# Threshold attention before a squared-ReLU feed-forward: shared last-query units, two units at a time, 64x64 tiles

## The chip, the cores and the metric

The kernel runs on one core of a Trainium2 chip. The metric is the device time of one execution in microseconds, from the first instruction to the last. The kernel before takes 1461.16 us (median of three runs, 1460.78 to 1461.53).

The engines are named as in the profile: PE (TensorE, matrix products and transposes), PEld (its weight loads), DVE (VectorE), ACT (ScalarE), POOL (GpSimd) and SP, which here only issues DMA. Each takes its own instructions in the order in which they were written and waits at semaphores for the others. Products land in PSUM, eight banks of 512 fp32 columns on 128 partitions; PE, DVE and ACT reach it here, POOL works on SBUF alone.

## What is computed

The reference has two parts. Attention, over 8 batches, 8 heads, 576 positions and head size 64:

```python
scores = scale * np.matmul(q, k.transpose(0, 1, 3, 2))
thresh = np.max(scores, axis=-1, keepdims=True) - tau
scores = np.where(scores >= thresh, scores, -1000000000.0)
scores = scores - np.max(scores, axis=-1, keepdims=True)
attn = np.exp(scores)
attn = attn / (np.sum(attn, axis=-1, keepdims=True) + 1e-09)
return np.matmul(attn, v).astype(np.float32)
```

Its result is laid out as 4608 tokens of 512 features, and a feed-forward follows: `h = max(x @ w_in, 0)`, then `(h * h) @ w_out`, with 2048 hidden features. q, k, v and the result are fp32, and the two weight matrices arrive as 64-bit floats. The number 576 is four and a half times 128, so each head has 64 queries and 64 keys left over after four full blocks; much of the kernel, and the whole change, is about these.

## The kernel before, in words

**The order of the work** is written out by hand. Attention comes first and ends when the first matmul of the feed-forward (`hidden_layer`, L708) starts; then come the nine steps of the hidden layer and the nine of the output layer (L843). The feed-forward uses a two-level scheme of sums in place of some products (`inner`, `sums`, `prepare_x`); the change leaves it alone, apart from when its weights are prepared during attention.

**Attention** goes over 32 pairs of heads. A pair has five slots (`slots`): four of 128 queries with both heads, and one of the last 64 queries, in which the two heads lie on the two halves of the partitions. That makes 160 slots. A slot passes these steps:

- `scores_rest` (L340): one full-array product of the 128 queries with a block-diagonal matrix of the last 64 keys of both heads (`kdiag`), into the middle of a three-bank PSUM tile `sc`, of which there are two.
- `scores` (L355): one product of 64 rows by 512 keys for each head. The heads sit on rows 0 to 63 and 64 to 127 of the array; in the last slot each uses 64 columns too.
- `softmax`: a negated maximum for each head on DVE (L366), the threshold on POOL (L371), exp on ACT (L378), mask and sum in one DVE instruction (L383), the small constant added on POOL (L387), a reciprocal on DVE (L389), and the normalization on POOL (L398).
- `transposes`: four 128-key transposes for each head (L439), and one for the last keys of both (L414), each into a PSUM bank that ACT then copies to SBUF (L441, L418). All use `bank`, a pool of two banks.
- `values` (L469, L474): ten products of 64 stationary columns, each head on its own half of the array's columns, with the last keys' values block diagonal (`vdiag`). They wait in `pending`, and the next slot's `rest` copies them out with its own transposes.

`turn` (L306) transposes q and k of the next pair once in five slots, and `turn_last` (L317) their last 64 rows. `load` and `load_v` fetch q, k and v. `slot(n)` interleaves all of this: it turns the weights of slot n-1, multiplies the values of slot n-2, and writes the scores of slot n+3, while `stage` and `second` step the softmaxes of n+1 and n+2. The engines run through the resulting queues; PE meets scores, values and transposes of different slots in a fixed sequence.

Between them lie the **weights of the feed-forward**: they arrive as 64-bit floats; `fetch` loads 32 raw tiles, `convert1` to `convert6` turn each into fp32 by ACT, POOL and DVE, and `sums_step` adds them on POOL, one addition a slot. `starts`, `OUT_SUMS`, `IN_FIRST` and `IN_SUMS` say in which slot each begins. The result x of attention goes to DRAM (`give_x`, `later`, `ask`), from where `load_x` takes it.

Of the kernel before, what the change touches and what calls it, by code (L numbers as in the profile page):

```python
# [48 lines left out]
def kernel(  # L49
# [74 lines left out]
    vdiag = [sb.tile([P, P], FP32, tag=f"vdiag{i}") for i in range(2)]  # L124
    kdiag = [sb.tile([P, P], FP32, tag=f"kdiag{i}") for i in range(2)]
    for t in vdiag + kdiag:
        nc.gpsimd.memset(t[:, :], 0.0)

# [137 lines left out]
    loaded, loaded_v, turned, weights = {}, {}, {}, {}  # L266

    def load(i):
        b, hp = pairs[i]
        h = 2 * hp  # L270
        qn = sb.tile([P, FULL, P], FP32, tag="qn", name="qn")
        kn = sb.tile([P, FULL, P], FP32, tag="kn", name="kn")

        rn = sb.tile([P, P], FP32, tag="rn", name="rn")

        for src, dst, order, rows in ((q, qn, "(t p) d -> p t d", 0), (k, kn, "(p t) d -> p t d", REST)):

            queue = nc.scalar if i == 0 and src is k else nc.sync
            for j in range(2):
                queue.dma_start(out=dst[:, :, ds(j * D, D)], in_=src[b, h + j, 0:MAIN, :].rearrange(order, p=P))  # L280
            queue.dma_start(
                out=rn[ds(rows, REST), :].rearrange("p (j d) -> p j d", j=2),
                in_=src[b, h : h + 2, MAIN:S, :].rearrange("j p d -> p j d"),
            )
        loaded[i] = (qn, kn, rn)

    def load_v(i):
        b, hp = pairs[i]
        h = 2 * hp
        va = sb.tile([P, 2, FULL, D], FP32, tag="va", bufs=2, name="va")  # L290
        vd = vdiag[i % 2]
        nc.sync.dma_start(out=va[:, :, :, :], in_=v[b, h : h + 2, 0:MAIN, :].rearrange("j (p t) d -> p j t d", p=P))
        for j in range(2):
            nc.sync.dma_start(out=vd[ds(j * D, D), ds(j * D, D)], in_=v[b, h + j, MAIN:S, :])
        loaded_v[i] = (va, vd)

    def turn(i):

        qn, kn, rn = loaded.pop(i)
        qT = sb.tile([P, S], FP32, tag="qT", bufs=2, name="qT")  # L300
        kT = sb.tile([P, S], FP32, tag="kT", bufs=2, name="kT")
        turning[i] = (qT, kT, rn)
        for nat, to in ((qn, qT), (kn, kT)):
            pt = bank([P, FULL, P], "pqk")
            for t in range(FULL):
                nc.tensor.transpose(pt[:, t, :], nat[:, t, :], ident[:, :])  # L306
            flat, to = pt[:, :, :].rearrange("p t m -> p (t m)"), to[:, 0:MAIN]
            if nat is kn:
                nc.scalar.copy(to, flat)
            else:  # L310
                nc.scalar.activation(out=to, in_=flat, func=AF.Identity, scale=qscale[:, :])
            yield

    def turn_last(i, pt):

        qT, kT, rn = turning.pop(i)
        nc.tensor.transpose(pt, rn[:, :], ident[:, :])  # L317

        def then():
            nc.scalar.activation(out=qT[:, MAIN:S], in_=pt[:, 0:REST], func=AF.Identity, scale=qscale[:, :])  # L320
            nc.scalar.copy(kT[:, MAIN:S], pt[:, REST:P])
            for j in range(2):
                rows = ds(j * D, D)
                nc.gpsimd.tensor_copy(out=kdiag[i % 2][rows, ds(j * REST, REST)], in_=kT[rows, MAIN:S])
            turned[i] = (qT, kT)
            if i + 1 < len(pairs):
                load(i + 1)
# [3 lines left out]
    def scores_rest(i, t):  # L331

        sc = sc_pool.tile([P, 3 * BANK], FP32, tag="sc", name="sc")
        if t < FULL:
            qT, _ = turned[i]
            to = sc[:, MAIN:S]
            to = bass.AP(tensor=to.tensor, offset=to.offset, ap=[to.ap[0], [2 * BANK - S, 2], [1, REST]])
            nc.tensor.matmul(to, qT[:, ts(t, P)], kdiag[i % 2][:, :], start=True, stop=True)  # L340
        return sc

    def scores(i, t, sc):

        qT, kT = turned[i]
        m = BLK[t]  # L350
        for k0, n in ((0, MAIN),) if t < FULL else ((0, MAIN), (MAIN, REST)):
            for j in range(2):
                rows = ds(j * D, D)
                to = sc[rows, ds(k0, n)] if t == FULL else sc[:, ds(j * 2 * BANK, n)]
                nc.tensor.matmul(to, qT[rows, ds(t * P, m)], kT[rows, ds(k0, n)], start=True, stop=True)  # L355

    def softmax(i, t, sc):

        nj = 2 if t < FULL else 1
        at = (0, 2 * BANK - REST)[0:nj]  # L360
        sm = sb.tile([P, 2], FP32, tag="sm", bufs=3, name="sm")
        nmx = sb.tile([P, 2], FP32, tag="nmx", bufs=3, name="nmx")
        thr = sb.tile([P, 2], FP32, tag="thr", bufs=3, name="thr")
        w = sb.tile([P, 2 * S], FP32, tag="w", bufs=3, name="w")
        for j in range(nj):
            nc.vector.tensor_reduce(  # L366
                out=nmx[:, j : j + 1], in_=sc[:, ds(at[j], S)], axis=AXIS.X, op=ALU.max, negate=True
            )
            if j == nj - 1:

                nc.gpsimd.tensor_scalar(  # L371
                    out=thr[:, 0:nj], in0=nmx[:, 0:nj], scalar1=-1.0, scalar2=tau_p[:, :], op0=ALU.mult, op1=ALU.subtract
                )
            yield
        for j in range(nj):
            if j:
                yield
            nc.scalar.activation(  # L378
                out=w[:, ts(j, S)], in_=sc[:, ds(at[j], S)], func=AF.Exp, bias=nmx[:, j : j + 1], scale=1.0
            )  # L380
        for j in range(nj):
            yield
            nc.vector.scalar_tensor_tensor(  # L383
                out=w[:, ts(j, S)], in0=sc[:, ds(at[j], S)], scalar=thr[:, j : j + 1], in1=w[:, ts(j, S)],
                op0=ALU.is_ge, op1=ALU.mult, accum_out=sm[:, j : j + 1],
            )
        nc.gpsimd.tensor_scalar(out=sm[:, 0:nj], in0=sm[:, 0:nj], scalar1=1e-9, scalar2=None, op0=ALU.add)  # L387
        yield
        nc.vector.reciprocal(out=sm[:, 0:nj], in_=sm[:, 0:nj])  # L389
        if t == FULL:  # L390

            normalize(w[:, S : S + REST], w[:, MAIN:S], sm[:, 0:1])
        for j in range(nj):
            normalize(w[:, ts(j, S)], w[:, ts(j, S)], sm[:, j : j + 1])
        weights[i, t] = w

    def normalize(out, w, r):
        nc.gpsimd.tensor_scalar(out=out, in0=w, scalar1=r, scalar2=1.0, op0=ALU.mult, op1=ALU.mult)  # L398

    def transposes(n):  # L400

        if n < 0:
            return
        i, t = slots[n]
        w = weights.pop((i, t))
        wT = sb.tile([P, 2, FULL, P], FP32, tag="wT", bufs=2, name="wT")
        weights[i, t] = wT
        at = ds(0, BLK[t])

        def rest():  # L410
# [8 lines left out]
            else:  # L419
                if n_:  # L420
                    nc.scalar.copy(xr[:, 0, 0:n_], pt[:, 0, 0:n_])
# [625 lines left out]
```

## Time and profile before

| what | value |
|---|---|
| time, median of three | 1461.16 us |
| span of the profiled execution | 1460.0 us |
| first scores product (L355) starts | 10.5 us |
| last scores product starts | 648.6 us |
| first feed-forward product (L708) starts | 661.5 us |
| one slot of attention, from two pairs in 40 us | 4.00 us |
| mask, mean (L383) | 814 ns, x288 |
| maximum, mean (L366) | 756 ns, x288 |
| exp, mean (L378) | 746 ns, x288 |
| 512-column copy of weights, mean (L441) | 592 ns, x256 |
| normalization, mean (L398, 576 columns) | 752 ns, x288 |
| granted TensorE clock | 1.00 |

How to read it: the profile lists groups of instructions by line, engine and shape with a mean duration. An engine starts its next instruction before the last has ended, so the distance between two starts in the timeline is the better measure of what an instruction costs its engine, and the mean tells when its result is there. Matmuls are pipelined, and their ends are modelled; only their starts are measured. The timeline merges runs of alike instructions into one line: start, duration, engine, line of the kernel, what it writes and reads, count, and, in brackets, how long the engine had been idle and for whom.

### The profile page before, as it was taken

The numbers are of one execution on the slowest core, as the hardware profiler recorded it, in microseconds if no ns is written. First come the engines' busy times: TensorE is split into PE (matmuls) and PEld (weight loads), VectorE is DVE, ScalarE is ACT, GpSimd is POOL, SyncE is SP. The second block draws the span as 40 slices with busy tenths as digits, with TensorE's granted clock in tenths as the row PEclk, the third lists the DMA queues.
The fourth block names the chain that finished last, engine by engine and source line by source line (L and its number), as shares of the span: only waits on it lengthen the run. The fifth ranks groups of instructions, "written<-read, shape, count | busy, mean of one in ns | idle before, by whom it ended". The sixth has DMA issues, their size and how long they took to land. (4 is left out here: it accounts for less than half of the span.)

```text
span 1460.0 us, 35321 instructions
## 1 busy us (share of the span) xinstructions
PE 1435.8 (98%) x12914; PEld 1216.0 (83%) x12914; DVE 1007.1 (69%) x2152; ACT 890.8 (61%) x1792; POOL 1053.6 (72%) x1318
## 2 busy tenths in 40 slices
PE   8999999999999999999999999999999999999998
PEld 5666666666666666669999999999999999999998
DVE  4888766777887667666777877778765656545663
ACT  5888777778887777774766666767543333323330
POOL 3777788778888888773556655666777777777775
PEclk9999999999999999999999999999999999999999
DMA  4443223676442222202433233433984442244411
GB/s 126 106 129 109 66 65 115 189 229 183 122 123 75 54 54 65 64 26 63 145 124 132 94 109 123 146 123 119 387 303 146 145 131 78 89 138 145 145 30 30
DMA packets 212957, 176.90 MB, mean 121 GB/s; under 512 B 99888, under 2 KB 161328, under 8 KB 212784
## 3 DMA queue, kind: packets, MB, share of 16 engines
q1 hardware_dynamic: 210896, 174.09, 38.0%
q8 instruction: 102, 1.67, 0.5%
q10 hardware_dynamic: 1888, 0.56, 0.2%
q14 instruction: 71, 0.58, 0.1%
HBM read 105.12 MB, written 69.47 MB: 120 GB/s over the span
## 5 line engine op out<-in xcount | busy, mean ns | idle before, releaser
L133 POOL TENSOR_TENSOR arena<-arena 128x512 f32<-128x512 f32 (+1 forms) x314 | 376.8, 1223 | 250.4 <-DVE arena L133 221.1
L708 PE MATMUL ph<-arena,w 128*128 128x128 f32 x3528 | 396.6, 275 | 1.5 <-DVE arena L133 0.5
L708 PEld LDWEIGHTS ph<-arena,w 128*128 128x128 f32 x3528 | 394.7, 192 | 3.4 <-DVE arena L133 2.9
L843 PE MATMUL po<-w,arena 128*128 128x128 f32 x3528 | 396.6, 275 | 0.3
L843 PEld LDWEIGHTS po<-w,arena 128*128 128x128 f32 x3528 | 394.9, 192 | 2.0 <-issue 1.6
L133 DVE TENSOR_TENSOR arena<-ph,arena 128x512 f32<-128x512 f32 x378 | 255.4, 688 | 93.0 <-PE ph L708 52.3
L366 DVE TENSOR_REDUCE arena<-sc 128x1 f32<-128x576 f32 x288 | 217.6, 756 | 127.9 <-PE sc L355 127.7
L383 DVE SCALAR_TENSOR_TENSOR arena<-sc,arena 128x576 f32<-128x576 f32 x288 | 224.6, 814 | 7.2 <-ACT arena L378 6.9
L398 POOL TENSOR_SCALAR arena<-arena 128x576 f32<-128x576 f32 (+1 forms) x320 | 223.6, 709 | 7.4 <-DVE arena L389 2.6
L133 DVE TENSOR_TENSOR arena<-po,arena 128x128 f32<-128x128 f32 x378 | 108.2, 290 | 169.5 <-PE po L843 168.3
L654 ACT COPY c<-arena 128x512 f32<-128x512 f32 (+1 forms) x303 | 172.9, 580 | 62.9 <-DVE arena L130 56.8
L378 ACT ACTIVATE arena<-sc,arena 128x576 f32<-128x576 f32 x288 | 200.6, 746 | 10.7 <-DVE arena L366 6.4
L439 PEld LDWEIGHTS pwT<-ident,arena 128*128 128x128 f32 x1152 | 128.6, 141 | 76.1 <-issue 29.9
L355 PE MATMUL sc<-arena 64*128 64x512 f32 (+2 forms) x768 | 184.5, 571 | 1.1 <-DVE arena L383 0.7
L130 POOL TENSOR_TENSOR arena<-arena 128x512 f32<-128x512 f32 (+1 forms) x138 | 175.0, 1268 | 9.7
L439 PE MATMUL pwT<-ident,arena 128*128 128x128 f32 x1152 | 180.9, 280 | 0.5 <-ACT arena L441 0.3
L130 DVE TENSOR_TENSOR arena<-arena,c 128x512 f32<-128x512 f32 (+1 forms) x267 | 174.9, 663 | 7.5 <-ACT c L654 6.6
L441 ACT COPY arena<-pwT 128x512 f32<-128x512 f32 x256 | 151.5, 592 | 42.0 <-PE pwT L439 31.7
L469 PE MATMUL pvR<-arena 128*64 128x128 f32 (+1 forms) x2560 | 163.3, 268 | 5.1 <-ACT arena L441 0.7
L469 PEld LDWEIGHTS pvR<-arena 128*64 128x64 f32 x2560 | 127.8, 136 | 34.8 <-issue 20.8
L687 ACT ACTIVATE arena<-arena 128x512 f32<-128x512 f32 x144 | 90.0, 625 | 76.8 <-POOL arena L133 76.7
L622 ACT COPY arena<-po 128x128 f32<-128x128 f32 x63 | 16.7, 265 | 179.0 <-PE po L843 177.1
(56 smaller groups left out, 1158.1 us busy)
## 6 DMA issues: line engine op xcount, KB each, us to landing
g<-arena SPq DMA_DIRECT2D x144, 256.0 KB, 2.0
arena<-g SPq DMA_DIRECT2D x144, 256.0 KB, 4.5
w<-w SPq DMA_DIRECT2D x98, 256.0 KB, 4.9
out_dram<-arena SPq DMA_DIRECT2D x70, 128.0 KB, 2.3
arena<-in_q_dram SPq DMA_DIRECT2D x64, 128.0 KB, 2.7
arena<-in_v_dram SPq DMA_DIRECT2D x32, 256.0 KB, 2.8
arena<-in_moe_w_out_dram SPq DMA_DIRECT2D x16, 512.0 KB, 4.2
xT<-arena SPq DMA_DIRECT2D x128, 64.0 KB, 1.6
```

The source lines that it names most:

```text
L130: e.tensor_tensor(out=out, in0=x, in1=y, op=ALU.subtract)
L133: e.tensor_tensor(out=out, in0=x, in1=y, op=ALU.add)
L355: nc.tensor.matmul(to, qT[rows, ds(t * P, m)], kT[rows, ds(k0, n)], start=True, stop=True)
L366: nc.vector.tensor_reduce(out=nmx[:, j : j + 1], in_=sc[:, ds(at[j], S)], axis=AXIS.X, op=ALU.max, negate=True)
L378: nc.scalar.activation(out=w[:, ts(j, S)], in_=sc[:, ds(at[j], S)], func=AF.Exp, bias=nmx[:, j : j + 1], scale=1.0)
L383: nc.vector.scalar_tensor_tensor(out=w[:, ts(j, S)], in0=sc[:, ds(at[j], S)], scalar=thr[:, j : j + 1], in1=w[:, ts(j, S)], op0=ALU.is_ge, ...
L398: nc.gpsimd.tensor_scalar(out=out, in0=w, scalar1=r, scalar2=1.0, op0=ALU.mult, op1=ALU.mult)
L439: nc.tensor.transpose(pt[:, c, :], w[:, ds(j * (S + REST) + c * P, P)], ident[:, :])
L469: nc.tensor.matmul(pv[rows, :], va[:, j, c, :], wT[:, j, c, 0:n], start=(c == 0), stop=False, skip_group_check=True)
L654: nc.scalar.copy(c, y)
L708: nc.tensor.matmul(to[:, j, :], W_IN[m, k][:, ts(j, P)], of[k][:, m - 1, :], start=(not more and j == 0), stop=True, skip_group_check=True,)
L843: nc.tensor.matmul(to, g[:, j, :], w[:, j, :], start=(not more and j == 0), stop=(j == 3), skip_group_check=True)
```

## The change

Attention is rebuilt; the feed-forward's products are the same.

- **Units.** Two pairs together have nine units instead of ten slots: eight of 128 queries, and one that holds the last 64 queries of both pairs (`halves`), each with both heads. Every unit now has 128 rows in use for both heads. There are 144.
- **Periods.** `period(p)` takes two units, A = 2p and B = 2p+1, through scores, maximum and exp, masks and normalizes the two of the period before (a and b), and multiplies the values of the two before those (`values(m)`, m = p-2). There are 72, with two before and a few after to fill and to drain.
- **Keys and values** are read nine rows to a partition, so that a head's 576 keys are nine chunks of 64, and chunk c of both heads together gives one 128-row transpose. A unit has nine transposes, all alike, and `vdiag` is gone; `kdiag` stays for the scores of the last chunk. The weights lie in SBUF as [chunk, head, 64].
- **Quarter tiles.** `scores` splits the 128 queries in two: four products of 64 rows and 64 columns of the array, by 512 keys. `values` does the same: the head chooses the rows, the unit of the period the columns, 36 products a period. Each head writes its own PSUM bank.
- **Softmax.** One reduction takes the maxima of both heads. The threshold and the small constant move from POOL to DVE.
- **Fills.** The transposes of two units go into five banks (`FILLS`); the first two share the banks in which the values end, so one ACT copy takes both. The last is filled and copied in the next period, ahead of the values that use it. `wT` has one buffer of five banks instead of two of two; the PSUM pool keeps two banks, `sc` two tiles.
- **Queues.** A `turn` of q or k goes into each of most periods (`TURNS`). Conversions of the weights start once in a period, and three sums go into each.

The core of the diff:

```diff
+    units = []
+    for i in range(0, len(pairs), 2):
+        units += [((i + e,) * 2, t) for e in range(2) for t in range(FULL)]
+        units.append(((i, i + 1), FULL))
...
-    def scores(i, t, sc):
-        qT, kT = turned[i]
-        m = BLK[t]
-        for k0, n in ((0, MAIN),) if t < FULL else ((0, MAIN), (MAIN, REST)):
+    def scores(n, sc):
+        pair, t = units[n]
+        for c in range(2):
             for j in range(2):
-                rows = ds(j * D, D)
-                to = sc[rows, ds(k0, n)] if t == FULL else sc[:, ds(j * 2 * BANK, n)]
-                nc.tensor.matmul(to, qT[rows, ds(t * P, m)], kT[rows, ds(k0, n)], start=True, stop=True)
+                rows, at = ds(j * D, D), ds(c * HALF, HALF)
+                qT, kT = turned[pair[c]]
+                lhs = qT[rows, ds(t * P + c * HALF, HALF)] if t < FULL else last_q(pair[c])[rows, at]
+                nc.tensor.matmul(sc[at, ds(j * 2 * BANK, MAIN)], lhs, kT[rows, 0:MAIN], start=True, stop=True)
...
+        def top():
+            nc.vector.tensor_reduce(out=nmx, in_=both, axis=AXIS.X, op=ALU.max, negate=True)
+        def least():
+            nc.vector.tensor_scalar(
+                out=thr, in0=nmx, scalar1=-1.0, scalar2=tau_p[:, :], op0=ALU.mult, op1=ALU.subtract
...
+    FILLS = (
+        [(0, c) for c in range(3)], [(1, c) for c in range(3)],
+        [(0, c) for c in range(3, 7)], [(1, c) for c in range(3, 7)],
+        [(u, c) for c in (7, 8) for u in range(2)],
+    )
...
-        for c in range(FULL):
-            for j in range(2):
-                rows = ds(j * D, D)
-                nc.tensor.matmul(
-                    pv[rows, :], va[:, j, c, :], wT[:, j, c, 0:n], start=(c == 0), stop=False, skip_group_check=True
-                )
+    def values(m):
+        out = [bank([P, BANK], f"pv{j}") for j in range(2)]
+        x = wT.pop(m)
+        for c in range(CH):
+            for u in range(2):
+                for s, (i, _, count, row) in enumerate(halves(2 * m + u)):
                     for j in range(2):
+                        rows = ds(j * D, D)
+                        nc.tensor.matmul(
+                            out[j][ds(u * D, D), ds(row, count)], loaded_v[i][rows, c, :],
+                            x[rows, ds(AT_OF[u, c] + row, count)],
+                            start=(c == 0 and s == 0), stop=(c == CH - 1), skip_group_check=True,
+                        )
...
+        do(a, "mask", 0)
+        do(a, "mask", 1)
+        do(a, "over")
+        do(a, "inverse")
+        do(a, "normal", 0)
+        do(a, "normal", 1)
+        begin(A)
+        if has(A):
+            scores(A, sc[A])
+            softmax(A, sc[A])
+        convert3(begun(p - 1))
+        last = bank([P, BANK], "p4") if has(2 * m) else None
+        if last:
+            fill(m, 4, last)
+        if last:
+            filled(m, 4, last)
+        if g:
+            turn(g // 2, g % 2)
+        convert1(begun(p))
+        convert2(begun(p))
+        then = None
+        begin(B_)
+        if g and g % 2:
+            then = turn_last(g // 2, sc[B_][:, SPARE : SPARE + P])
+        do(b, "mask", 0)
+        do(b, "mask", 1)
+        if has(B_):
+            scores(B_, sc[B_])
+            softmax(B_, sc[B_])
+        do(A, "top")
+        do(b, "over")
+        do(b, "inverse")
+        do(b, "normal", 0)
+        do(b, "normal", 1)
+        pv = values(m) if has(2 * m) else None
+        do(A, "power", 0)
+        do(A, "least")
+        do(A, "power", 1)
+        do(B_, "top")
...
+        pt0 = first(0, pv)
+        pt1 = first(1, pv)
+        do(B_, "power", 0)
+        if pt0:
+            filled(m + 1, 0, pt0, pv)
+        if pt1:
+            filled(m + 1, 1, pt1, pv)
...
+        do(B_, "power", 1)
...
+        pt2 = other(2)
+        if pt2:
+            filled(m + 1, 2, pt2)
+        pt3 = other(3)
+        if pt3:
+            filled(m + 1, 3, pt3)
```

Here `begin` takes a score tile and writes the last keys' scores, `fill` transposes into a bank, `filled` is ACT's copy of it, `top` is the joint maximum, `power` an exp, `over` and `inverse` the small constant and the reciprocal, `normal` the normalization on POOL.

## The prediction

> **What bounds the kernel now.** I read the page first, then the windows, then the timeline of one stretch of attention engine by engine, then the waits of the weight loads there.
>
> ```profile
> PE 1435.8 (98%) x12914; PEld 1216.0 (83%) x12914; DVE 1007.1 (69%) x2152; ACT 890.8 (61%) x1792; POOL 1053.6 (72%) x1318
> ...
> PE   8999999999999999999999999999999999999998
> PEld 5666666666666666669999999999999999999998
> ```
>
> PE is busy throughout, but the weight loads show two halves: tenths of 6 in the first 18 slices (attention), 9 after it (the feed-forward). In the second half the matmuls are back to back and nothing is changed. So only attention matters. Its lengths, from the timeline: the first scores (L355) start at 10.5 us and the feed-forward (L708) at 661.5 us; what follows takes 1461.2 - 661.5 = 799.7 us and stays.
>
> ```profile
> 560.00:600.00 40.00, 39.39 (x365) 26.21 (x366) 27.59 (x65) 28.96 (x62) 32.34 (x55) 1.00 0.24 61
> 600.00:640.00 40.00, 39.40 (x365) 26.23 (x366) 27.59 (x65) 28.95 (x62) 32.37 (x55) 1.00 0.19 46
> ```
>
> These windows (PE, PEld, DVE, ACT, POOL) hold two head pairs, ten slots, each: 40.0 us, so 4.00 us a slot, with DVE and ACT near 70%. Ends of matmuls are modelled, so I take costs from start to start:
>
> ```profile
> 302.46 1.13 PE L355 MATMUL sc<-arena 64*128 64x512 f32 x4
> 303.52 0.66 PE L439 MATMUL pwT<-ident,arena 128*128 128x128 f32 x4
> ...
> 305.30 0.60 PE L439 MATMUL pwT<-ident,arena 128*128 128x128 f32 x4
> 305.92 1.19 PE L355 MATMUL sc<-arena 64*64 64x512 f32 x8
> 307.04 0.66 PE L439 MATMUL pwT<-ident,arena 128*128 128x128 f32 x4
> 307.63 1.10 PE L469 MATMUL pvR<-arena 128*64 128x128 f32 x16
> 308.56 0.39 PE L474 MATMUL pvR<-arena 128*64 128x128 f32 x4
> 308.88 0.33 PE L414 MATMUL pvR<-ident,arena 128*128 128x128 f32 x1
> ```
>
> An fp32 matmul is two instructions here (2560 at L469 for 1280 products); a transpose is one. Four transposes cost 0.44 us (301.03 to 301.47 in the same view), 0.109 each. Twenty value instructions take 307.63 to 308.88, 1.25 us. Four instructions of 512 columns take 1.06 us; at 0.109 per 128 columns they would need 1.74 one by one, so the two row tiles run together (2 x 0.436 = 0.87), and about 0.19 is the change into tiles and out again.
>
> Sum for a pair: 50 transposes 5.45, rest scores 0.87, values 4 x 1.09 + 0.55 = 4.9, scores 4 x 0.87 + 0.98 = 4.5, ten changes of tiling (scores and values in each slot) at 0.2 = 2.0: 17.7 us, 3.54 a slot. Measured 4.00. So 0.46 us a slot, 11%, is PE waiting in order:
>
> ```profile
> PEld pwT L439 <- POOL arena L387: 11.4, 15, 0.8
> ...
> PEld pqk L306 <- ACT arena L378: 9.1, 12, 0.8
> ...
> PEld pvR L469 <- ACT arena L309: 5.8, 16, 0.6
> ```
>
> These (200 to 520 us) are waits for the two-bank PSUM pool to be copied out by ACT and for other engines.
>
> The other engines by the same reading:
>
> ```profile
> 300.55 0.82 DVE L383 SCALAR_TENSOR_TENSOR arena<-sc,arena 128x576 f32<-128x576 f32 x1
> ...
> 301.29 0.76 DVE L366 TENSOR_REDUCE arena<-sc 128x1 f32<-128x576 f32 x1
> ...
> 301.96 0.16 DVE L389 RECIPROCAL arena<-arena 128x2 f32<-128x2 f32 x1
> ...
> 302.38 1.39 ACT L378 ACTIVATE arena<-sc,arena 128x576 f32<-128x576 f32 x2
> ```
>
> A mask occupies DVE 0.74 us, a reduction 0.67, an exp ACT 0.64 (1.39 for two); a 512-column copy 0.48, with 0.59 to its end.
>
> **What the Trainium skill says.** "TensorE: Matmul & The Clock Gate", Part 3: tiles in different row and column groups run at once (sixteen tiles measured at 10.6 times one). It also says that matmuls start and end strictly in order. The trace shows two tiles at once, not four. "TensorEngine Tiling (Array Packing)", Key Properties: changing the tiling mode drains TensorE; the 0.19 above agrees. The same page, Gotcha 1: row tiles must write to different PSUM banks at once. The new code obeys, since head j has its own bank in scores and values; no trace here shows the opposite. "VectorE: DVE Perf Modes", The DRAIN you can't avoid: a result read by the next DVE instruction needs a semaphore or an instruction between. So I charge a dependent small operation its whole duration, 0.16, plus about 0.05.
>
> **The change part by part.**
>
> *Fewer units.* Two pairs take 9 units, not 10 slots: 144 units in 72 periods of two, where 160 slots stood. A half-filled slot cost almost what a whole one costs on PE.
>
> *PE per period.* Rest scores 4 x 0.109 = 0.44, plus 0.05 for the accumulation in every ninth unit. Scores A: four products of 64x64 by 512 columns, eight instructions; four at once is 2 x 0.436 = 0.87, plus the change 0.2 = 1.07. Transposes of the last chunk 0.44. Turn of q or k 0.38 (62 of 72 periods), its rest 0.05. Scores B and values share one tiling, so one change: 0.87 + 0.2 + values. Values are 36 products, 72 instructions; four at once is 18 x 0.109 = 1.96. Transposes 6 + 8 at 0.109 = 1.53. Sum 0.49 + 1.07 + 0.44 + 0.43 + 3.03 + 1.53 = 6.99. Two old slots were 7.08: the arithmetic per period stays, two of four tiling changes go (0.4) and denser values save 0.2, but two full units replace an average with half-filled slots.
>
> The unknown is the quarter tile: four at once is one bound, two at once the other (values 3.92, scores 1.74 each, +3.7 a period). I take four: the column halves and the row halves each run together in the trace, and the four operands are disjoint.
>
> *Waits on PE.* Two banks rotate. The fill pY needs the bank of the first fill copied: after `first(0)` and `first(1)`, 0.33 each, the copy of the first begins some 0.25 behind its transposes (those from 303.52 on are through by 304.01, ACT's copy starts at 304.27), ends 0.59 later, and frees PE 0.05 after that (304.24 to 304.29), so PE waits 0.89 - 0.33 = 0.56; the next fill waits 0.05 more behind the second copy. Behind it stand the next period's scores. Total 7.6. The other transposes find their banks free: scores or turns lie between.
>
> *DVE per period.* Masks 4 x 0.74 = 2.96; two joint reductions of 1152 at 0.60 + 0.60 + 0.07 = 1.27 each; six small operations (two of three come over from POOL), about 0.2 each; sum 6.7, beside PE's 7.6. In the 32 periods with weight conversion two integer operations add 1.1, and the mask that frees the score bank comes late by about 0.3 us: 0.13 on average.
>
> *ACT.* Exps 4 x 0.64, fills 5 x 0.48, turns 0.7, conversions 1.2 in 32 of 72: 6.2 on average; it hides. POOL loses its small operations (0.6 us a slot of hand-overs, a wait in the fences above) and keeps four normalizations at 0.72 and up to three weight sums of 1.25: 6.6; the normalization of B ends about 0.7 us before its transpose.
>
> *DMA.* Keys come in more pieces of 256 bytes, values in fewer. The next q is asked for about 2.5 us into a period and needed 1.7 us into the next, 6.9 us later; five issues at 0.4 and a landing of 2.7 make 4.7. Nothing.
>
> *Sum.* Period 7.6 + 0.13 = 7.75 with rounding for the ten without a turn. Start 10.5, drain 9.5 (before: 13.0 from the last scores; now masks 1.5, normalization 1.9, fills 3.1, values and copies 3), so the feed-forward starts at 10.5 + 72 x 7.75 + 9.5 = 578, and the end is at 578 + 799.7 = **1378 us**. Break-even is a period of 8.9.
>
> **The rivals.**
>
> *Coupling (24%).* DVE at full durations (masks 0.90 with their accumulator reads, reductions 2 x 0.76, small 0.25, conversions 0.6) would need 8.7. The loop of unit B, scores, maximum, exp, mask, scores, passes three in-order engines and is itself about 7 us, so slips may not average out: a period of 8.0 to 8.7, middle 8.3: **1417 us**. Late q loads (2 us for 16 pairs, 32 us) would land here too. For it: 0.46 us of such waits per slot now. Against: DVE has 0.9 us spare.
>
> *Quarter tiles two at a time (13%).* 7.75 + 3.7 = 11.45: 20 + 824 + 800 = **1644 us**, slower. For it: the strict order, and both passes of one product follow each other in the program. Against: two tiles already overlap despite that.
>
> *No waits (7%).* Copies keep up, 7.1 a period: **1331 us**.
>
> **How the numbers follow.** The forecast has 56%. Coupling reaches slower than before only beyond 8.9, 2 of its 24. Faster 0.56 + 0.22 + 0.07 = 0.85, slower 0.14, same 0.01. The range leaves out the quarter-tile case and thin ends: 7.2 a period gives 1338, 8.6 gives 1439.
>
> **What would show it.** Right: the two-unit period 7.6 to 7.9 us; 72 value instructions start within about 2.0 us and eight score instructions within 0.9; PE's largest wait is for ACT's fill copies; the feed-forward starts near 578 with its 0.11 per instruction unchanged. Wrong: value instructions over 0.04 us apart (quarter tiles), score matmuls waiting for the mask (coupling), or turns waiting for a q load.

## The result, and the profile after

The kernel after the change takes 1419.5 us (median; 1419.2 to 1422.8), the kernel before 1461.3 us in the same session (1460.8 to 1461.5): a ratio of 0.9718, 95% interval 0.9705 to 0.9732. It is faster by 41.7 us, half of the 83 us forecast. The profiled execution spans 1417.6 us. The first scores start at 11.19 us and the feed-forward (now L745) at 618.9, where 578 was forecast; what follows takes 798.7 us in the profile (798.5 before). So nearly the whole error lies in attention: 40.9 us.

The page shows the engines' busy time, and PE's busy tenths and granted clock in 40 slices:

```profile
PE 1353.1 (95%) x15882; PEld 1189.4 (84%) x15882; DVE 1068.7 (75%) x2280; ACT 850.5 (60%) x1578; POOL 947.7 (67%) x967
...
PE   4999999889999999999999999999999999999998
...
PEclk8999999999999999999999999999999999999999
```

PE is busy for 83 us less, and its share falls from 98 to 95%: about half of that came back as idle time. That 83 is also the gain that was forecast is chance: the prediction's own sums of PE's work differ by 63 us (160 slots of 3.54 against 72 periods of 6.99), and busy time counts modelled ends. DVE now has more work than before (1068.7 against 1007.1 us) in a shorter time. The first slice says 4, and slices 8 and 9 say 8: two places to look at.

One period without disturbance, PE alone, from scores A to scores A:

```profile
299.60 1.09 PE L378 MATMUL sc<-arena 64*64 64x512 f32 x8
...
300.62 0.66 PE L446 MATMUL p<-ident,arena 128*128 128x128 f32 x4
...
301.11 0.60 PE L330 MATMUL pqk<-ident,arena 128*128 128x128 f32 x4
301.55 0.39 PE L365 MATMUL sc<-arena 128*128 128x128 f32 x2
301.86 1.09 PE L378 MATMUL sc<-arena 64*64 64x512 f32 x8
...
302.77 2.15 PE L464 MATMUL pv<-arena 64*64 64x128 f32 x72
...
304.85 0.87 PE L446 MATMUL pv<-ident,arena 128*128 128x128 f32 x6
...
306.12 1.14 PE L446 MATMUL pY<-ident,arena 128*128 128x128 f32 x8 [0.39 <-ACT arena L453]
...
307.10 0.39 PE L365 MATMUL sc<-arena 128*128 128x128 f32 x2
...
307.41 1.09 PE L378 MATMUL sc<-arena 64*64 64x512 f32 x8
```

From start to start: scores A 1.02, last fill 0.49, turn 0.44, rest 0.31, scores B 0.91, values 2.08, six transposes and the wait for the copy 1.27, eight transposes 0.98, rest 0.31; together 7.81 us. Eight score instructions in 0.91 and 72 value instructions in 2.08: four quarter tiles do run at once. The single starts, which the view merges, say it directly: the value instructions start in groups of four, 6 to 7 ns apart, one group every 109 ns.

The start, ACT and PE (the bracket at the end of a line is the engine's idle time before it, and who ended it):

```profile
22.54 0.65 ACT L203 ACTIVATE arena<-arena 128x512 f32<-128x512 f32 x1 [7.26 <-DMA arena<-in_moe_w_out_dram]
...
23.64 2.62 ACT L401 ACTIVATE arena<-sc,arena 128x576 f32<-128x576 f32 x4
26.73 0.77 PE L365 MATMUL sc<-arena 128*128 128x128 f32 x2 [9.84 <-DVE arena L406]
27.43 1.99 PE L378 MATMUL sc<-arena 64*64 64x512 f32 x8
```

ACT takes its instructions in order. The first weight conversion (L203) stands ahead of the first exps (L401) and waits for its weights until 22.5 us; the exps wait behind it, the masks behind them, and PE stands for 9.84 us. Afterwards the eight score instructions take 1.91 us from start to start instead of 1.02 (29.34 - 27.43): the granted clock was 0.5 from 20.4 us for 10.2 us.

In the middle, where sums of output weights are stored, SyncE's issues (SPq) with ACT and PE:

```profile
245.40 4.73 SPq L510 DMA_DIRECT2D w<-w  x7
...
250.23 0.40 SPq L294 DMA_DIRECT2D arena<-in_q_dram  x1
...
255.38 0.63 PE L330 MATMUL pqk<-ident,arena 128*128 128x128 f32 x4 [1.68 <-DMA arena<-in_q_dram]
...
261.73 1.07 ACT L453 COPY arena<-pv 128x512 f32<-128x512 f32 x2 [2.23 <-DMA xT<-arena]
...
262.37 1.63 PE L446 MATMUL pY<-ident,arena 128*128 128x128 f32 x8 [2.35 <-ACT arena L453]
```

Seven stores are issued in a row, the loads of q come behind them, and PE waits for q. The store of x (xT) is late too; its source shares the one buffer wT with the fills, so ACT's copy waits for it and PE for ACT.

Later, where sums run beside attention, DVE and POOL show something that the prediction had priced at 0.2 us:

```profile
315.06 1.27 POOL L132 TENSOR_TENSOR arena<-arena 128x512 f32<-128x512 f32 x1
315.10 1.25 DVE L412 TENSOR_SCALAR arena<-arena 128x2 f32<-128x2 f32 x1
...
316.39 0.17 DVE L415 RECIPROCAL arena<-arena 128x2 f32<-128x2 f32 x1
```

L412 adds a constant to two numbers per partition. At 302.16, with POOL idle, it took 0.16 us; here it started 0.04 us into a POOL addition and took 1.25, ending with it. Over the trace, 85 of its 144 instances start while no POOL operation runs, and all of these are short; all 43 that last over 0.26 us started during one, 39 of them during an addition of weights. Another 16 started during a POOL operation and stayed short, ten of them during a normalization. The reciprocal L415 started during a POOL operation 30 times, 20 of them during an addition, and never took over 0.168 us. The Trainium skill, "SBUF — State Buffer", Who interferes with whom, fits this: a tensor_scalar can take the port pair that DVE shares with GpSimd, where its operands meet certain conditions, and then whoever comes second is blocked for the whole instruction. The prediction did not use that page.

What PE waited for, over the whole execution (us in total, times, longest):

```profile
PE pY L446 <- ACT arena L453: 34.5, 72, 2.5
...
PE sc L365 <- DVE arena L406: 13.1, 10, 9.8
...
PE pqk L330 <- DMA arena<-in_q_dram: 3.5, 4, 1.7
```

The first is the steady wait for the copy of the first fill. The other two are the prediction's own signs of being wrong: scores that wait for a mask (9.8 us of it at the start, 3.3 us in nine waits later) and turns that wait for q.

Where the 40.9 us stand, by the starts of scores A in the 72 periods (forecast 7.75 each): first scores 0.7 late; periods 0 and 1 take 25.3, +9.8; the next 69 take 564.1 instead of 534.8, +29.3; the last period and drain +1.1. The experiments divide the 29.3.

### The profile page after: what moved, and what is told of

Its sections match the earlier page's. It is cut to its first block, busy times and chain, and to the rows that moved or that the text cites. A ratio compares the mean times of both kernels' runs of the same rounds, so it can differ in the third digit from the quotient of the medians.

```text
span 1417.6 us, 40533 instructions
## 1 busy us (share of the span) xinstructions
PE 1353.1 (95%) x15882; PEld 1189.4 (84%) x15882; DVE 1068.7 (75%) x2280; ACT 850.5 (60%) x1578; POOL 947.7 (67%) x967
## 4 chain that ended last, share of the span: by engine, by line
PE 52%; DMA 2%; DVE 1%; ACT 1%; POOL 1%; issue 0%; DVEq 0%; POOLq 0%; SPq 0%
PE po L880 28%; PE ph L745 24%; DVE arena L135 1%; DMA w<-w 1%; POOL arena L135 1%; DMA g<-arena 0%; ACT arena L659 0%; ACT arena L724 0%; DVEq L135 0%; POOLq L135 0%; ACT arena L725 0%; SPq L726 0%; SPq L963 0%
## 5 line engine op out<-in xcount | busy, mean ns | idle before, releaser
L745 PE MATMUL ph<-arena,w 128*128 128x128 f32 x3528 | 396.7, 275 | 1.9 <-DVE arena L135 0.8
L745 PEld LDWEIGHTS ph<-arena,w 128*128 128x128 f32 x3528 | 394.8, 192 | 3.8 <-DVE arena L135 3.1
L418 POOL TENSOR_SCALAR arena<-arena 128x576 f32<-128x576 f32 x288 | 212.0, 752 | 139.6 <-DVE arena L396 69.4
L401 ACT ACTIVATE arena<-sc,arena 128x576 f32<-128x576 f32 x288 | 206.3, 751 | 23.8 <-DVE arena L393 13.4
L393 DVE TENSOR_REDUCE arena<-sc 128x2 f32<-128x1152 f32 x144 | 195.1, 1355 | 32.4 <-PE sc L378 31.5
L464 PEld LDWEIGHTS pv<-arena 64*64 64x64 f32 x5760 | 154.9, 133 | 37.0 <-issue 21.8
L378 PE MATMUL sc<-arena 64*64 64x512 f32 x1152 | 160.4, 628 | 0.0
L464 PE MATMUL pv<-arena 64*64 64x128 f32 (+1 forms) x5760 | 157.8, 259 | 0.7 <-ACT arena L453 0.7
L659 ACT COPY arena<-po 128x128 f32<-128x128 f32 x63 | 16.7, 265 | 178.9 <-PE po L880 177.1
L446 PE MATMUL pY<-ident,arena 128*128 128x128 f32 x576 | 82.9, 287 | 34.5 <-ACT arena L453 34.5
L446 PEld LDWEIGHTS pY<-ident,arena 128*128 128x128 f32 x576 | 60.6, 141 | 56.7 <-ACT arena L453 51.6
L132 POOL TENSOR_TENSOR w<-w 128x512 f32<-128x512 f32 x77 | 96.9, 1277 | 2.4
```

The costliest lines, as they stand in the source:

```text
L132: e.tensor_tensor(out=out, in0=x, in1=y, op=ALU.subtract)
L378: nc.tensor.matmul(sc[at, ds(j * 2 * BANK, MAIN)], lhs, kT[rows, 0:MAIN], start=True, stop=True)
L393: nc.vector.tensor_reduce(out=nmx, in_=both, axis=AXIS.X, op=ALU.max, negate=True)
L401: nc.scalar.activation(out=w[:, :, j, :], in_=of(j), func=AF.Exp, bias=nmx[:, j : j + 1], scale=1.0)
L418: nc.gpsimd.tensor_scalar(out=w[:, :, j, :], in0=w[:, :, j, :], scalar1=rs[:, j : j + 1], scalar2=1.0, op0=ALU.mult, op1=ALU.mult)
L446: nc.tensor.transpose(pt[:, ds(P * (i + (f < 2)), P)], w[:, c, :, :].rearrange("p j d -> p (j d)"), ident[:, :])
```

## The experiments

The theory after reading the trace: four separate causes, (a) weight conversion ahead of exps at the start, (b) DVE's small operations behind POOL, (c) the burst of stores in SyncE's queue with x in a shared buffer, (d) PE's own sum, 0.2 us a period too small. The rival was coupling without any single cause: three in-order engines near their limit, so that mending one point moves nothing. All kernels compare with the kernel before, 1461 to 1462 us in each session.

In the table, "first two" is the sum of periods 0 and 1; the other columns are mean periods in us, all of one profiled execution of each kernel: output weights converted (2 to 17), their sums and stores (18 to 33), input weights converted (34 to 51), their sums (52 to 67). Where the weights come two periods later, these stretches lie two periods later too, and stores reach into period 36. Kernels that do the same in a stretch agree within 0.01 us outside the stores (the change and x in two places; three mended and 7 stores of 49), but four kernels with the same start take 18.1 to 20.5 us in the first two periods.

| kernel | time | ratio, interval | first two | 2-17 | 18-33 | 34-51 | 52-67 |
|---|---|---|---|---|---|---|---|
| the change | 1419.5 | .9718 (.9705-.9732) | 25.3 | 7.94 | 8.51 | 8.22 | 8.13 |
| weights two periods later | 1414.6 | .9675 (.9659-.9692) | 19.3 | 8.01 | 8.41 | 8.43 | 8.01 |
| no small tensor_scalars | 1416.1 | .9688 (.9674-.9703) | 25.7 | 8.13 | 8.37 | 8.08 | 7.98 |
| no constant added | 1414.6 | .9681 (.9667-.9696) | 23.2 | 7.95 | 8.67 | 8.07 | 7.99 |
| stores spread | 1420.9 | .9726 (.9710-.9742) | 26.6 | 7.98 | 8.37 | 8.32 | 8.09 |
| x in two places | 1418.8 | .9706 (.9690-.9722) | 25.1 | 7.94 | 8.51 | 8.22 | 8.13 |
| three mended | 1406.7 | .9625 (.9610-.9639) | 19.5 | 8.01 | 8.45 | 7.95 | 7.98 |
| three mended, warm, spread | 1406.8 | .9620 (.9599-.9640) | 16.7 | 7.96 | 8.31 | 8.29 | 7.98 |
| three mended, GpSimd stores | 1412.9 | .9669 (.9652-.9685) | 18.2 | 7.97 | 8.73 | 8.09 | 7.98 |
| three mended, 7 stores of 49 | 1399.1 | .9565 (.9546-.9584) | 20.5 | 8.00 | 8.01 | 7.94 | 7.98 |
| three mended, two queues | 1402.8 | .9613 (.9587-.9638) | 18.1 | 7.96 | 8.08 | 8.14 | 7.98 |

**Weights two periods later.** The first weight conversion starts in period 2 instead of 0; all later weight work moves with it.

```diff
-    starts = {m: m for m in range(16)}
+    starts = {m + 2: m for m in range(16)}
```

> Starts the conversion of the weights in period 2, not 0, and moves what follows by two periods; nothing is left out. Theory (the start): in period 0 the exps stand on ScalarE behind a conversion that waits 7.3 us for its weight tile, so period 0 takes 16.2 us; it should take about 8 to 9, and the whole 1411 to 1413 us. Rival (the start is long because q and k of the second pair land late, or because TensorE is cold): period 0 stays above 14 us and the time within 2 us of 1419.5.

Measured 1414.6 us. ACT and PE in the same place:

```profile
15.33 1.36 ACT L401 ACTIVATE arena<-sc,arena 128x576 f32<-128x576 f32 x2
17.61 1.37 ACT L401 ACTIVATE arena<-sc,arena 128x576 f32<-128x576 f32 x2 [0.92 <-DVE arena L393]
19.45 0.77 PE L365 MATMUL sc<-arena 128*128 128x128 f32 x2 [3.30 <-DVE arena L406]
```

The exps start at 15.3 instead of 23.6 and PE's gap falls from 9.84 to 3.30 us. Period 0 shrinks from 16.24 to 8.74, but period 1 grows from 9.04 to 10.57 with the clock still low (0.5 from 18.5 us for 6.8 us), and period 34, into which stores now fall, takes 10.63. The cause of the start is shown; 5 of its 10 us come back as time.

**No small tensor_scalars.** The addition of 1e-9 to a sum that is at least 1 is left out (here and in the kernels below that are called mended), and the threshold is computed by ACT.

```diff
+    nc.vector.tensor_scalar(out=ntau[:, :], in0=tau_p[:, :], scalar1=-1.0, scalar2=None, op0=ALU.mult)
...
         def least():
-            nc.vector.tensor_scalar(
-                out=thr, in0=nmx, scalar1=-1.0, scalar2=tau_p[:, :], op0=ALU.mult, op1=ALU.subtract
-            )
+            nc.scalar.activation(out=thr, in_=nmx, func=AF.Identity, bias=ntau[:, :], scale=-1.0)
...
         def over():
-            nc.vector.tensor_scalar(out=sm, in0=sm, scalar1=1e-9, scalar2=None, op0=ALU.add)
+            pass
```

> Takes the two small tensor_scalars of a unit off VectorE: the threshold goes to ScalarE, and the addition of 1e-9 to the sum is left out (the sum is at least 1, so the addition changes no fp32 sum). Theory (shared access): these two wait out GpSimd's long additions, 42 us beyond their quick durations in all, and the mask, and so the score bank, comes late; the periods with weight sums fall from 8.51 and 8.13 us to about 8.0, the time to 1407 to 1413 us. Rival (TensorE sets the period and VectorE has room): 1417 to 1420 us.

Measured 1416.1 us, 3.4 us faster, between the theory's range and the rival's. Both stretches with input weights improve (8.22 to 8.08, 8.13 to 7.98), but the first conversion stretch gets slower (7.94 to 8.13): there the first six transposes with their wait for ACT's copy take 1.44 us where they took 1.30, so ACT, which now computes the threshold beside its conversions, comes later.

**No constant added.** Only the addition of 1e-9 is left out; the threshold stays on DVE.

> Leaves out only the addition of 1e-9 to the sum (at least 1, so no fp32 sum changes); the threshold stays on VectorE. Theory (TensorE sets the plain period, VectorE's small operations cost only where GpSimd adds weights): plain periods stay at 7.8 and 8.05 us, those with sums and the second conversions lose 0.1 to 0.2, the time falls by 4 to 7 us to 1412 to 1416. Rival (the two operations share in the plain period): plain periods fall by 0.2 and the time by over 12 us.

Measured 1414.6 us, 4.9 us faster by the medians. The three small operations by groups (busy us, mean ns), first in the kernel of the change:

```profile
L412 DVE TENSOR_SCALAR arena<-arena 128x2 f32<-128x2 f32 x144 | 53.2, 370 | 2.5
L396 DVE TENSOR_SCALAR arena<-arena,tau_p 128x2 f32<-128x2 f32 x144 | 41.9, 291 | 1.5
L415 DVE RECIPROCAL arena<-arena 128x2 f32<-128x2 f32 x144 | 23.9, 166 | 10.5 <-DVE arena L412 0.5
```

then with the constant left out:

```profile
L396 DVE TENSOR_SCALAR arena<-arena,tau_p 128x2 f32<-128x2 f32 x144 | 48.3, 335 | 1.5
...
L415 DVE RECIPROCAL arena<-arena 128x2 f32<-128x2 f32 x144 | 23.1, 161 | 5.1
```

53.2 us of L412 go, L396 gets 6.4 us longer: part of the waiting moves to the next tensor_scalar. Of 47 us of DVE work, 4.9 us show in the time. The rest lay beside PE. In the trace, periods 34 to 67 get 5.0 us shorter and those with stores 2.7 us longer; another 2.1 us come from the first two periods, where L412 is never held up, and so are not the edit's. PE's nine later waits for a mask are gone.

**Stores spread.** At most three stores of weight sums at each of the two places in a period where SyncE is given stores.

```diff
+        for _ in range(min(3, len(stores))):
+            to, from_ = stores.popleft()
+            nc.sync.dma_start(out=to, in_=from_)
```

> Issues the stores of the summed output weights three at a time, after the x writes, where seven stood in one row; nothing is left out. Theory (the DMA issue queue): seven stores hold the queue for 5 us, so q loads and x writes come late and periods around 250 to 265 us stretch to 12.3 us; the 16 periods with output-weight sums fall from 136 us to about 128, the time to 1411 to 1413 us. Rival (those periods are long for the small tensor_scalars alone): within 2 us of 1419.5.

Measured 1420.9 us, no gain: a miss. The longest period of the stretch (12.34 us) is gone, but periods of 9.97, 10.18, 9.40 and 9.40 stand in its place: ACT waits for the store of x three times, 6.0 us in all. Spreading by six a period only moves the lateness.

**Values head by head.** The same 36 products, but the loop over the heads is the outermost in `values`, so that two products of one bank follow each other and not four disjoint tiles.

```diff
-        for c in range(CH):
-            for u in range(2):
-                for s, (i, _, count, row) in enumerate(halves(2 * m + u)):
-                    for j in range(2):
+        for j in range(2):
+            for c in range(CH):
+                for u in range(2):
+                    for s, (i, _, count, row) in enumerate(halves(2 * m + u)):
```

> The 36 value products in the order of all of one head and then all of the other, so that two 64x64 tiles, not four, are named in turn; the same products. Theory (four tiles run at once only when four are named in turn): the 72 instructions take about 4.0 us where they took 2.1, a period grows by 1.9 us less what it hides, and the time goes to 1530 to 1560 us. Rival (order does not matter, TensorE looks far enough ahead, or the values are hidden beside the other engines): 1419 to 1440 us.

Measured 1517.9 us, ratio 1.0388 (1.0372 to 1.0403): slower than the kernel before. The values of one period and what follows:

```profile
307.29 3.73 PE L464 MATMUL pv<-arena 64*64 64x128 f32 x72
310.95 0.87 PE L446 MATMUL pv<-ident,arena 128*128 128x128 f32 x6
```

From start to start 3.66 us instead of 2.08: close to the price of two tiles at a time that the prediction had worked out (36 x 0.109 = 3.92), without any change in the arithmetic. The instructions start in pairs, one pair every 109 ns; only in the middle, where the heads change, do three steps have four starts, which makes the 3.66. The period's mean is 9.57 us, and the sums and stores no longer show in it (9.55 to 9.57 in all four stretches). So the order of the loop alone decides whether the change gains 42 us or loses 56. The Trainium skill, "TensorE: Matmul & The Clock Gate", Part 3, has matmuls start and end strictly in the order of the program. A record does not say which of the two passes of a product it is, so these traces neither confirm nor refute that; they show that the prediction's fear, two passes of one tile that keep the next tile out, did not come true with four tiles named in turn.

**x in two places.** The part of the first two fills that carries x lies at alternating columns of wT, so a fill need not wait for the store of x.

```diff
-        a, z = P if f < 2 and not pv else 0, BANK if has(2 * m) else P
-        nc.scalar.copy(wT[m][:, ds(f * BANK + a, z - a)], pt[:, a:z])
+        a, z, to = 0, BANK, base(f)
+        if f < 2 and m % 2 == 0:
+            a, z = 0 if pv else P, BANK if has(2 * m) else P
+        elif f < 2:
+            a, z, to = 0 if has(2 * m) else 3 * P, BANK if pv else 3 * P, base(f) + P
+        nc.scalar.copy(wT[m][:, ds(to + a, z - a)], pt[:, a:z])
```

> Gives the x part of each fill two places in SBUF in turn (columns before and behind the transposed weights), so that ScalarE's copy of new values need not wait until the x write of the period before has landed; nothing is left out. Theory (late x writes hold the copy, the copy holds the PSUM bank): the waits of ScalarE's fill copy for the xT write, 4.5 to 6 us around 250 to 310 us in three traces so far, go, and with them 2.0 to 2.5 us of TensorE's wait each time; that stretch shortens by 6 to 9 us, the time falls to 1410 to 1414 us. Rival (these periods are long for late q loads and GpSimd): within 2 us of 1419.5.

Measured 1418.8 us: a miss. ACT's wait for the store of x is gone from the stretch, but PE now waits there for q, 5.3 us in three waits. The buffer was not what set the time; what stood behind it took its place.

**Three mended.** Weights two periods later, no constant, x in two places.

> Conversions two periods later, no addition of 1e-9, x in two places, together. If the three costs add: 1419.5 less 5 (measured for the first), less about 5, less 6 to 9, so 1399 to 1404 us. If the second and third hide the same waits: 1405 to 1409.

Measured 1406.7 us, 12.8 us faster than the change alone. Apart they gave 4.9, 4.9 and 0.7, together 10.5: in the time they about add up, so the second of the two expected ranges came: the third edit was worth far less than the 6 to 9 us assumed. The periods 2 to 70 do not add up: single edits change their sum by +1.9, -2.2 and +0.2 us, the three together by -6.9. Outside the stores the periods are now 7.95 to 8.01. In the stretch one of 15.09 us remains; SyncE and PE there:

```profile
258.87 4.60 SPq L519 DMA_DIRECT2D w<-w  x7
263.57 0.59 SPq L294 DMA_DIRECT2D arena<-in_q_dram  x1
...
266.38 0.58 SPq L294 DMA_DIRECT2D arena<-in_q_dram  x1
...
269.08 1.09 PE L330 MATMUL pqk<-ident,arena 128*128 128x128 f32 x4 [4.43 <-DMA arena<-in_q_dram]
```

The first piece of q is issued as the burst ends, the second 2.8 us later behind pieces of k, and PE has waited 4.43 us. The wait costs more than itself: the granted clock was 0.5 from 267.8 us for 6.8 us, and the turn, the rest scores, scores B and values of this period take 2.7 us longer than usual.

**Three mended, warm, spread.** Besides, 20 dummy transposes in each of the periods 0 and 1 keep PE's clock up, and the stores are spread over SyncE's two places.

> The three edits, the spread stores, and 20 idle transposes of the identity in each of the first two periods, whose results nothing uses. Theory (cold clock at the start): the granted clock stays at 1.00 through the first periods, which shorten by 2 to 4 us against the three edits alone; the spread stores give 0 to 3 us once the x copy no longer waits. So 2 to 7 us below the run of the three edits. Rival: no difference over 1 us.

Measured 1406.8 us (1401.9 to 1409.0): nothing gained. The first two periods fall to 16.7 us, near the 15.5 forecast, with the clock at 1.00 through them, but single periods of 10.37 and 13.75 us stand elsewhere. In the second PE waits 4.3 us for q. In the first it waits 2.5 us for a mask, and that one stands behind a threshold (L396) that lasted 3.86 us, until three POOL additions in a row had ended, more than the one instruction that the page cited above speaks of.

**Stores from GpSimd.** With the three mended, GpSimd issues each store right behind its addition.

```diff
-            later.append((w_dram[m, k_][:, :], W_OUT[m, k_][:, :]))
+            nc.gpsimd.dma_start(out=w_dram[m, k_][:, :], in_=W_OUT[m, k_][:, :])
```

> The three mended edits stay (1406.7 us before this edit; sums-out periods 18 to 33 mean 8.45 us against about 7.95 in plain stretches, so some 8 us stand there). The 49 stores of the weight sums are issued by GpSimd right behind the additions that make them, no longer by SyncE, so that loads of q and k and stores of x do not stand behind them in SyncE's queue; the bytes moved are the same. Theory A (SyncE's queue of issues is what makes q late): sums-out mean near 8.05, 1400 us. Rival B (the DMA engines are full, whoever issues): no change, 1405 to 1408 us, PE still waits for q loads there. Rival C (issuing on GpSimd delays its normalizations): slower, 1410 or more, with waits of PE for GpSimd.

Measured 1412.9 us. PE has no wait for q left between 165 and 330 us, though the same bytes go in the same stretch; instead it waits for GpSimd's normalization. From the timeline of POOL and, in a fence of its own, the waits of 165 to 300 us (us in total, times, longest):

```profile
245.40 3.78 POOL L262 DMA_DIRECT2D w<-w  x7
```

```profile
PE pv L449 <- POOL arena L418: 9.8, 9, 2.2
```

Both A and C were right in part: it was SyncE's queue that made q late, and seven issues of 0.54 us each are no cheaper where the normalizations stand behind them. (Longer periods also give a load more time; the last experiment, with the same bytes and shorter periods, leaves PE no wait for q either.)

**Seven stores of 49.** With the three mended, 42 stores are left out, and the feed-forward reads the first seven sums in their place, so its output is another.

> The three mended edits stay. Only the seven sums of the first outer index are stored; the other 42 stores are left out, and the feed-forward reads the first seven in their place, so the output is not the reference's. Theory A and rival B both expect the sums-out periods to fall to about 8.05 us and 1400 us, since neither issues nor bytes of the 42 stores are left (10.5 MB less). If the stretch stays at 8.4, the stores are not its cause and GpSimd's additions are (their port, or normalizations that come late).

Measured 1399.1 us. The stretch falls from 8.45 to 8.01 us a period, as all others: the stores were all that was special in it. GpSimd's additions, which stay, do not show.

**Stores from two queues.** With the three mended, each of the two places in a period gives one store to SyncE and one to ScalarE, of sums ordered at an earlier place.

```diff
+        for queue in (nc.sync, nc.scalar):
+            if due:
+                to, from_ = due.popleft()
+                queue.dma_start(out=to, in_=from_)
+        due.extend(stores)
+        stores.clear()
```

> The three mended edits stay (1406.7 us). The 49 stores are spread over the periods at up to four each, half a period or more after their addition was ordered, one by SyncE and one by ScalarE at each of the two places where stores are issued, so that SyncE has 1.2 us of them in a period instead of 4.6 us at once, ScalarE has as much in a stretch where it has no conversions, and GpSimd has none. Theory (a burst in SyncE's queue makes the q loads late, 4.4 us of PE's waiting once and 7 us over the stretch; the bytes do not matter): the sums-out periods fall from 8.45 to about 8.05 us, 1400 us, near the run with seven stores only (1399.1 us). Rival (spreading only moves the lateness to other periods, as in the run that spread them on SyncE alone, or ScalarE's copies come late behind its issues): 1405 to 1410 us, with single periods above 9 us left.

Measured 1402.8 us (1401.5 to 1409.8), the fastest median apart from the one that leaves stores out. SyncE's queue in the stretch:

```profile
254.24 1.03 SPq L523 DMA_DIRECT2D w<-w  x2
255.37 0.51 SPq L294 DMA_DIRECT2D arena<-in_q_dram  x1
```

The stretch is at 8.08, but three periods of 9.2 to 9.6 us remain (two of them after 34), so some of it is only moved. PE waits for no load there, but in all three ScalarE stands idle for 2.1 to 2.8 us up to a copy for PE and issues a store within that time: the copy stands behind the store, and the store is itself late. What it waits for is not shown. The run's interval overlaps that of the three mended without this edit: the traces show the stretch shorter by 5.9 us, the times do not yet settle a gain.

## Why the prediction was wrong

The direction and the mechanism of the gain were right, the size was twice what came. The step that failed is the sum: a period of 7.75, a start of 10.5 and nothing for DMA. The 40.9 us divide as follows. In the run with three mended the 69 periods from 2 to 70 take 557.2 us instead of 564.1, and with seven stores 550.0; the forecast was 534.8.

- **PE's own sum: 15.2 us** (550.0 - 534.8, 0.22 a period). With seven stores, where most disturbances are out, the mean period by the terms of the prediction is: scores A 1.03 for 1.07, last fill 0.50 for 0.44, turn 0.38 for 0.38, rest scores with the last transposition 0.75 for 0.54, scores B and values 3.02 for 3.03, fourteen transposes with their wait 2.29 for 2.14. That is 7.97 for 7.60. The largest miss is at the rest scores: in the period shown above, two instructions that need 0.22 take 0.31 ahead of quarter tiles, twice a period. A pair of changes into quarter tiles and out costs about 0.25, where 0.2 was charged: this 0.09, and 0.12 to 0.15 at the tiles (1.02 for 0.87, 2.08 for 1.96). The eight transposes take 0.98 for 0.87; why is open. Of the 0.37 by which 7.60 was too small, 0.15 was made up by luck. The 0.13 for weight conversions was too much: with them, periods 2 to 17 take 8.00, hardly more than the rest. And 7.73 was rounded up for the ten periods without a turn, which should have brought it down: they take 7.63, against 7.82 with a q turn (medians). A k turn takes 8.15: it has the last transposition, 0.11, and about half of these periods the second rest product of a ninth unit, 0.22, both charged as 0.05 on average.
- **The start: 10.5 us** (0.7 and 9.8). "ACT: it hides" holds for sums over a period, not for the order in it. The prediction added conversions as work and did not ask what their first instruction waits for and what is queued behind it. Its start of 10.5 us, and two plain periods, assumed that the pipeline fills without a stop. With the conversions two periods later the first two periods took 18.1 to 20.5, and with PE kept busy besides 16.7, near the 15.5 forecast.
- **"DMA: Nothing": 7.2 us** (557.2 - 550.0). The prediction compared 6.9 us of time with 4.7 of loading, on a free queue. It did not put the seven stores of a weight sum, 4.0 to 5.5 us, ahead of the q load in the queue. The kernel before issues the same rows of seven, the first at 241.9 us in 3.9 us, so its trace had shown them. One of the prediction's rivals had the right mechanism ("Late q loads (2 us for 16 pairs, 32 us)") and put it at 24% together with others.
- **Small DVE operations, the x buffer and the later weights: 6.9 us** (564.1 - 557.2, the three edits together in these periods). "Six small operations about 0.2 each" was 0.37 and 0.29 in the mean for the two tensor_scalars, and 1.26 and 1.40 at worst.
- **The drain: 1.1 us.**

Right: quarter tiles four at a time (2.08 us, "about 2.0"); eight score instructions within 0.91 ("0.9"); the wait for the copies of the first fills, 0.61 forecast, 0.6 measured (1.27 less six transposes of 0.109), and the largest steady wait of PE; the feed-forward unchanged; the case of two tiles at a time, slower than before, when it was made to happen. Fewer units and fewer changes of tiling were not tried by themselves, so how the gain divides among them and the quarter tiles is not shown.

The coupling rival gave 1417 us, close to the result, with periods of 8.3; leaving out the first two, they average 8.18. That its number is so close is largely luck: 15.2 us are PE's own sum and 10.5 the start, and it had neither. But it was right in part. In periods 2 to 70 single edits change little (+1.9, -2.2 and +0.2 us) and three together bring back 6.9 us: where one late thing is mended, another takes its place, as q did when the wait for the store of x was gone. Part of this coupling has a name, DVE's small operations behind POOL, which delay the masks and so the scores. How the 6.9 divides between DVE, the buffer and the later weights stays open.

## What to carry to other kernels

Sums of busy time per period say whether an engine can hide, not whether it will: for every in-order queue (ACT, and SyncE's issues above all) ask what the first instruction of a new kind waits for and what stands behind it, most of all in the first periods and where work comes in bursts. Charge a change of tiling on both sides. Name independent quarter tiles in turn in the program; the loop order is worth more here than the whole change.

## What the runs showed of the hardware

- Four 64x64 tiles run at once when the program names them in turn: 72 instructions of 128 columns take 2.08 us from the first start to what follows, starting in fours every 109 ns; and 3.66 us, mostly starting in pairs, when the program names only two tiles (one head) in turn.
- A tensor_scalar of two fp32 numbers per partition on DVE (L412) lasts 0.16 us when no GpSimd operation runs and up to 1.26 us when it starts behind an addition of 512 columns; once, in the warm kernel, another (L396) was held for 3.86 us, by three additions in a row. A reciprocal of the same size is not held up (30 cases, at most 0.168 us).
- Seven issues of 256 KB stores in a row hold SyncE for 4.0 to 5.5 us, and GpSimd for 3.8 to 3.95; single ones on ScalarE take 0.33 to 0.36 each.
- Eight score instructions take 1.91 us from start to start at a granted clock of 0.5, against 1.02; PE's waits of 9.84 us at the start and of 4.43 us for a late q load came with 10.2 and 6.8 us at that clock.
